# An attention kernel with an MLP behind it: a new order model, free choice of engine for copies, and zero-padded means

## The chip, the cores and the metric

The kernel runs on one core of one Trainium2 chip. The metric is the device time of the whole program in microseconds (us), median of three executions. The core has five engines that work side by side and wait for one another through semaphores: TensorE (PE in the profile, with its weight loads PEld), VectorE (DVE), ScalarE (ACT), GpSimd (POOL) and SyncE (SP, which here issues most DMAs). Matmul results go to PSUM; this kernel uses four tiles of two banks there: duo0, duo1, hps and ops.

## What is computed

Two attentions over the same q, k and v (8 batches, 8 heads, 576 positions, 64 per head) are added, and the sum goes through an MLP with a SiLU.

```python
q_d = q.reshape(B, H, Sd, 4, D).mean(axis=3)          # the same for k_d, v_d: 144 means of four rows
out_d = sm_attn(q_d, k_d, v_d)                         # softmax attention over the 144 means
out_up = np.repeat(out_d, 4, axis=2)
mask = np.abs(pos[:, None] - pos[None, :]) < 4         # a band of 7 positions
scores = np.where(mask, scale * q @ k.T, -1e9)
out_local = softmax(scores) @ v
x = (out_up + out_local)                               # (4608 tokens, 512)
h = x @ w_in                                           # 512 x 2048
out = (h * sigmoid(h)) @ w_out                         # 2048 x 512
```

## The kernel before

Heads are worked on in pairs (32 of them), two pairs make a quad (16). The names of the phases are those of the text that follows:

- c, T, o, m: cast q and k to bf16, transpose them (TQ, TK on PE for the first eight quads, by DMA for the other eight), copy into qT and kT, form the means qd and kd.
- S1, S2: scores. S1 and the first two matmuls of S2 are the band, in five windows of 128 keys; the rest of S2 are scores of the means.
- e1, e2, e3, k: exponentials on ScalarE into Pt (band) and Pd (means), and the band mask on VectorE.
- Z or ZD: sums of the exponentials on PE, for the softmax. The first four quads are "direct": ZD, the reciprocals and RB (a matmul that spreads them over the partitions) stay on chip. For the others the reciprocals rr go through DRAM (scr) and come back broadcast as Rb.
- VD or castv (cv): means of v, on PE for the direct quads, on GpSimd for the others, into vd.
- PV: the products with v; pa and pb multiply by Rb into xo, and ad adds the repeated mean part to the local part into xT on GpSimd.
- g1, th, st: the first MLP matmuls (hps), tanh, and the product into gT. g2, ob, out: the second MLP matmuls (ops), copy, store.

No order is written by hand. Every phase is a task of one engine, with the tasks that must come first; at build time a greedy scheduler keeps a model of when each engine and buffer is free, and takes the next task per engine by modelled start plus weights from a table. That fixes each engine's instruction stream; on the chip every engine runs its stream in order and waits on semaphores.

```python
def choose(eng):
    c = [(s, t) for t in Q[eng][:LOOK[eng]] for s in [start(eng, t)] if s is not None]
    if eng != "PE":
        ...
        return min(c, key=lambda x: P.ready(eng, x[1][3], ()) + TUNE.get(kind(x[1][0]), 0))
    lead = min(max(ng1[0] - 16 - ng2[0], -16), 16)
    c = [(s + TUNE[kind(t[0])] + (0 if t[5] == mode[0] else TUNE["mode"]), s, t) for s, t in c]
    for k, r, w in mlp():
        s = max(P.free["PE"], P.ready("PE", r, w))
        c.append((s + TUNE[k] + (TUNE["lead"] * lead * (1 if k == "g1" else -1)) + ..., s, k))
    return min(c, key=lambda x: x[0])[1:] if c else None
```

The phases on PE that the change touches. `mm(..., m=...)` names the shape in which the array is used; the model charges 95 ns when it changes.

```python
vd = sb("vd", [128, 3, 2, 64], BF16, NVD)      # means of v: pair a of the quad on rows 64a to 64a+47
Pd = sb("Pd", [128, 2, 3, 72], BF16, NP_)      # exponentials of the means

def ph_S2(p):
    ...                                         # two matmuls of the band, m="row"
    for i in range(3):
        for b in range(2):
            for h in range(2):
                rows = slice(64 * h, 64 * h + 64)
                mm(D[rows, b, 120 + 72 * i:192 + 72 * i], kd[j][rows, i:i + 190:3],
                   qd[j][rows, 72 * b:72 * b + 72], ..., cost=18, m="diag")

def ph_Z(z):
    for c in range(8):                          # four at a time, 128 rows
        for o, m, a in hd:
            mm(D[o:o + 32, 0, 0:72], onesZ[:, c, :], Pt[m][:, a, 72 * c:72 * c + 72], ..., m="col4")
    for c in range(6):                          # four at a time, 48 rows
        for o, m, a in hd:
            mm(D[o:o + 32, 0, 0:72], onesZ[64 * a:64 * a + 48, 8 + c // 3, :],
               Pd[m][64 * a:64 * a + 48, c // 3, c % 3, :], ..., m="diag4")

def ph_PV(p):
    for c in range(5):                          # ten matmuls, two at a time, 128 rows
        for h in range(2):
            mm(o, vb[n][:, 5 * h + c, :], Pt[ms[h]][:, a, QB[c]:QB[c] + NQ[c]], ..., m="col")
    rows = slice(64 * a, 64 * a + 48)
    for i3 in range(3):                         # six matmuls, two at a time, 48 rows
        for h in range(2):
            mm(D[64 * h:64 * h + 64, 1, 120:264], vd[nd][rows, i3, h, :],
               Pd[ms[h]][rows, :, i3, :], ..., m="diag")
```

Each copy, cast and mean has one fixed engine:

```python
def castw(p):                                   # v to bf16
    P.op("ACT", lambda e: e.activation(vb[m][:, :, :], t, AF.Copy), ..., cost=730)
def cast(p, nm):                                # q, k: GpSimd (the first two pairs: VectorE and ScalarE)
    pool(lambda g: g.tensor_copy(dst, t), ..., cost=650)
pool_mean = tuple(range(2, 8))                  # heads whose k mean is on GpSimd, all others VectorE
```

At the very start VectorE fills constants, 16 of them memsets of four columns each:

```python
for t, c in ((onesS, 1.0), (foursS, 4.0)):
    fill(t[:, :, :], 0.0, [R("osb1")], 100, over=c > 1)
    for y in range(8):
        fill(t[:, y, 4 * y:4 * y + 4], c, [R("osb1")], 60, over=True)
```

Of the kernel before, what the change touches and what calls it, by code (L numbers as in the profile page):

```python
# [19 lines left out]
TUNE = {  # L20
    "tol": 0, "mode": 139, "lead": 77, "rep": 204, "g1": 606, "g2": 650, "TQ": -272, "TK": -88, "VD": -803,
    "S1": 101, "S2": -85, "ZD": -9384, "Z": -112, "RB": -6751, "PV": -220, "cw": 3143, "cv": -1199, "cq": 2831,
    "ck": 2297, "mask": -3629, "neg": -5281, "dm": 3751, "ones": 4973, "Tq": 6872, "Tk": 6930, "mq": -13444,
    "mk": -645, "e1": 916, "e2": -5624, "e3": 2392, "k": -751, "rc": -14116, "zs": -6353, "rb": 5365,
    "pa": -2169, "pb": -943, "th": 696, "st": 302, "ob": -445, "oq": -5037, "ok": -1684, "ad": -10747,
    "lqk": 5289, "lv": -8757, "lvq": 7893, "r": -4373, "b": 6923, "tq": -1508, "tk": 378, "out": 3873,
    "seq": ["lqk0", "lqk1", "lqk2", "lqk3", "lv1", "lv0", "w3", "lqk5", "lv2", "w0", "lqk4", "lv3", "lqk7",
            "lv5", "lv4", "w1", "lqk6", "w2", "w5", "lv7", "lv6", "w7", "w4", "w6", "lqk9", "lqk8"],
# [22 lines left out]
class Prog:  # L51
# [9 lines left out]
    def __init__(self):  # L61
        self.streams = {e: [] for e in self.ENGS}
        self.know = {e: {} for e in self.ENGS}
        self.dcount = {}
        self.free = {e: 0 for e in self.ENGS}
        self.rings = {"SP": [], "POOL": [], "ACT": []}
        self.ring_t = 0
        self.tag = ""
# [29 lines left out]
    def ready(self, eng, r, w):  # L98

        t = 0  # L100
        for x in r:
            for o in (x.last.values() if x.psum else x.writers):
                if o.eng != eng or o.dsem:
                    t = max(t, o.end + self.LATENCY[o.eng])
# [20 lines left out]
    def op(self, eng, fn, r=(), w=(), dma=None, cost=0, issue=450, tau=90):  # L125
# [31 lines left out]
        else:  # L157
            op.t0 = t
            self.free[eng] = op.end = t + cost * (1.3 if eng == "PE" and t < 40000 else 1)
        op.deps = [d for d, f in deps]  # L160
# [63 lines left out]
def bass_hourglass_attn__then__act_silu_kernel(  # L224
# [9 lines left out]
    with kctx:  # L234
# [22 lines left out]
        NST, NSTV, NVB, NVD, NP_, NR, NQT = 3, 2, 5, 3, 6, 4, 3  # L257
# [7 lines left out]
        vd = sb("vd", [128, 3, 2, 64], BF16, NVD)  # L265
# [8 lines left out]
        Pd = sb("Pd", [128, 2, 3, 72], BF16, NP_)  # L274
# [8 lines left out]
        onesZ = sb("onesZ", [128, 10, 32], BF16)  # L283
# [5 lines left out]
        rsb = sb("rsb", [128, 270], BF16, 2)  # L289
# [7 lines left out]
        direct, by_dma = tuple(range(4)), tuple(range(8, NQUAD))  # L297
        pool_mean = tuple(range(2, 8))
# [11 lines left out]
        def const_id():  # L310
            fill(id_bf[:, :], 0.0, [R("id")], 100)
            fill(mask_bf[:, :], 1.0, [R("mask")], 200)
            fill(band[:, :, :, :], 1.0, [R("band")], 60)
            for t, c in ((onesS, 1.0), (foursS, 4.0)):
                fill(t[:, :, :], 0.0, [R("osb1")], 100, over=c > 1)
                for y in range(8):
                    fill(t[:, y, 4 * y:4 * y + 4], c, [R("osb1")], 60, over=True)
            fill(Dm[:, :, :, 0:48], 1.0, [R("Dm")], 450)
            fill(Dm[:, :, :, 48:64], 0.0, [R("Dm")], 180)
            for i in range(2):  # L320
                fill(kd[i][:, 144:192], 0.0, [R(f"kdz{i}")], 60)
                fill(vq[32:64, i, :, :], 0.0, [R("vqz")], 800)
            fill(onesZ[:, :, :], 0.0, [R("ones")], 120)
            fill(onesZ[:, 0, 30:32], 1.0, [R("ones")], 60, over=True)
            pool(lambda g: g.affine_select(out=id_bf[:, :], in_=id_bf[:, :], compare_op=ALU.not_equal,
                                           fill=1.0, base=0, pattern=[[-1, 128]], channel_multiplier=1),
                 r=[R("id")], w=[R("id")])

        def const_z():

# [652 lines left out]
```

The softmax here doesn't subtract the row's maximum and nothing guards it: scores larger than these inputs give would overflow.

## Time and profile before

| | before |
|---|---|
| time, median of three | 391.66 us (391.12 to 392.93) |
| span of the profiled execution | 389.2 us |
| TensorE busy | 354.7 us, 91% |
| VectorE, ScalarE, GpSimd busy | 239.6, 215.1, 136.9 us |
| mean granted TensorE clock | 0.969 |
| moved by DMA | 66.77 MB, mean 172 GB/s |

The page of the profile describes one execution. Its slices cut the span in 40 equal parts of 9.7 us, with a digit for the busy share in tenths. The chain of waits goes back from the last instruction, at each step to what released it. Groups put together the instructions of one source line. All tasks of PE come from one helper line, so they are told apart by the names of their tiles: `hps<-xT,w_in_sb` is g1, `ops<-w_out_bf,gT` g2, `duo<-Pt,vb` and `duo<-Pd,vd` PV, `duo<-Pt,onesZ` Z. Matmuls are pipelined, so their durations overlap, and their distances are read from start to start. Two helper rows more, as an example of how such a group is read:

```profile
L754 DVE SCALAR_TENSOR_TENSOR gT<-th,hps 128x512 bf16<-128x512 f32 x136 | 92.5, 682 | 87.6 <-ACT th L752 87.5
L752 ACT ACTIVATE th<-hps 128x512 f32<-128x512 f32 x136 | 81.2, 598 | 107.5 <-PE hps L481 107.3
```

VectorE forms gT 136 times from hps, 92.5 us busy in all and 682 ns each; before these it stood idle 87.6 us, nearly all of it waiting for ScalarE's tanh, which in turn waits for PE.

### The profile page before, as it was taken

What the parts mean: (1) busy time and instruction counts of PE and PEld (TensorE: products, weight loads), DVE (VectorE), ACT (ScalarE), POOL (GpSimd) and SP (SyncE); (2) the same over time, 40 slices, a digit from 0 to 9 for tenths busy, and PEclk for the clock granted to TensorE, in tenths of its full rate; (3) what the DMA queues carried; (4) which work ended last, traced back from release to release, by engine and by line L of the source; (5) the groups of instructions that cost most, each with busy time, mean ns of one, the idle gap of its engine ahead of it and who ended that gap; (6) DMA issues with size and microseconds to landing.
All of it is one profiled execution on the core that took longest, in us unless ns stands there. A gap on an engine that the chain in (4) does not pass through costs nothing.

```text
span 389.2 us, 9061 instructions
## 1 busy us (share of the span) xinstructions
PE 354.7 (91%) x3841; PEld 221.3 (57%) x3880; DVE 239.6 (62%) x394; ACT 215.1 (55%) x364; POOL 136.9 (35%) x173
## 2 busy tenths in 40 slices
PE   0768599898999999999699999999999999999996
PEld 0656476655655556556455655666555656556542
DVE  6927477779978775986558899654363433334310
ACT  4756367666656765786167768463424344344321
POOL 7746826377624533452534622550040000000000
PEclk9968699999999999999879999999999999999999
DMA  8998997699999999999999999964000101101012
GB/s 260 323 319 232 177 250 191 193 250 240 262 247 274 194 252 242 285 219 220 173 256 239 195 174 226 211 156 108 27 29 32 51 27 44 39 27 53 29 54 81
DMA packets 87464, 66.77 MB, mean 172 GB/s; under 512 B 65152, under 2 KB 67200, under 8 KB 87424
## 3 DMA queue, kind: packets, MB, share of 16 engines
q1 hardware_dynamic: 83200, 59.90, 66.1%
q0 software_dynamic: 4224, 6.29, 7.3%
q8 instruction: 30, 0.49, 0.6%
q14 instruction: 10, 0.08, 0.1%
HBM read 53.67 MB, written 9.88 MB: 163 GB/s over the span
## 4 chain that ended last, share of the span: by engine, by line
PE 76%; DVE 15%; DMA 5%; issue 3%; ACT 1%; DVEq 0%; ACTq 0%
PE hps L481 31%; PE ops L481 30%; PE duo L481 12%; DMA qr<-qb 5%; DVE qd L519 3%; DVE qT L388 3%; DVE gT L754 2%; DVE qT L499 2%; DVE Pt L556 2%; PE duo L491 1%; DVE kd L519 1%; PE ops L491 0%; DVE rr L577 0%; DVE osb L308 0%; DVE duo L655 0%
## 5 line engine op out<-in xcount | busy, mean ns | idle before, releaser
L481 PE MATMUL hps<-xT,w_in_sb 128*128 128x512 f32 x544 | 169.9, 437 | 4.1 <-DVE gT L754 3.9
L754 DVE SCALAR_TENSOR_TENSOR gT<-th,hps 128x512 bf16<-128x512 f32 x136 | 92.5, 682 | 87.6 <-ACT th L752 87.5
L481 PE MATMUL ops<-w_out_bf,gT 128*128 128x512 bf16 x537 | 137.6, 383 | 3.9 <-issue 2.4
L752 ACT ACTIVATE th<-hps 128x512 f32<-128x512 f32 x136 | 81.2, 598 | 107.5 <-PE hps L481 107.3
L481 PEld LDWEIGHTS hps<-xT,w_in_sb 128*128 128x128 f32 x544 | 101.3, 193 | 34.5 <-DVE gT L754 7.1
L481 PEld LDWEIGHTS ops<-w_out_bf,gT 128*128 128x128 bf16 x576 | 47.5, 98 | 68.3 <-issue 25.5
L731 POOL TENSOR_TENSOR xT<-xo 128x576 fp32r<-128x576 f32 (+2 forms) x40 | 39.9, 1018 | 73.1 <-DVE xo L714 73.0
L433 POOL TENSOR_TENSOR vq<-vq 112x768 f32<-112x768 f32 x12 | 22.4, 1868 | 37.4 <-DMA vq<-in_v_dram 37.4
L556 DVE TENSOR_TENSOR Pt<-Pt,mask_bf 128x1152 bf16<-128x1152 bf16 x32 | 28.1, 884 | 11.8 <-ACT Pt L548 11.7
L775 ACT ACTIVATE osb<-ops 128x512 f32<-128x512 f32 x36 | 21.5, 597 | 25.1 <-PE ops L481 24.9
L532 ACT ACTIVATE Pt<-duo 128x912 bf16<-128x912 f32 x28 | 26.0, 928 | 6.4 <-PE duo L481 6.3
L519 DVE TENSOR_REDUCE qd<-qT 128x144 bf16<-128x576 bf16 x32 | 24.1, 752 | 5.7 <-PE duo L481 4.5
L422 POOL CAST qb<-qs 128x576 bf16<-128x576 f32 x27 | 18.8, 705 | 22.9 <-PE duo L491 17.8
L427 ACT ACTIVATE vb<-vs 128x640 bf16<-128x640 f32 x30 | 21.8, 738 | 4.0 <-DMA vs<-in_v_dram 2.4
L422 POOL CAST kb<-ks 128x576 bf16<-128x576 f32 x27 | 18.8, 708 | 8.4 <-DMA kr<-kb 6.6
L711 DVE TENSOR_TENSOR xo<-duo,Rb 128x456 f32<-128x456 f32 x29 | 18.0, 628 | 5.0 <-PE duo L481 2.9
L388 DVE TENSOR_REDUCE qT<-qr 128x576 bf16<-128x576 bf16 x16 | 18.6, 1162 | 3.4 <-DMA qr<-qb 3.4
L519 DVE TENSOR_REDUCE kd<-kT 128x144 bf16<-128x576 bf16 x26 | 18.9, 741 | 1.3 <-ACT kT L391 1.3
L391 ACT ACTIVATE kT<-kr 128x576 bf16<-128x576 bf16 x16 | 19.1, 1221 | 0.1
L550 ACT ACTIVATE Pd<-duo 128x432 bf16<-128x432 f32 x30 | 16.0, 534 | 0.0
L481 PE MATMUL duo<-qd,kd 64*64 64x72 bf16 x360 | 14.2, 218 | 0.8 <-DVE kd L519 0.8
L481 PEld LDWEIGHTS duo<-qT,kT 64*128 64x128 bf16 x284 | 8.1, 95 | 11.9 <-issue 6.3
(119 smaller groups left out, 297.6 us busy)
## 6 DMA issues: line engine op xcount, KB each, us to landing
vs<-in_v_dram SPq DMA_DIRECT2D x60, 160.0 KB, 5.2
out_dram<-osb SPq DMA_DIRECT2D x36, 256.0 KB, 2.0
Rb<-scr SPq DMA_DIRECT2D x24, 360.0 KB, 6.8
qs<-in_q_dram SPq DMA_DIRECT2D x29, 288.0 KB, 6.2
ks<-in_k_dram SPq DMA_DIRECT2D x29, 288.0 KB, 6.2
vq<-in_v_dram SPq DMA_DIRECT2D x24, 288.0 KB, 6.3
w_in_sb<-in_moe_w_in_dram POOLq DMA_DIRECT2D x4, 1024.0 KB, 8.2
w_out_bf<-in_moe_w_out_dram POOLq DMA_DIRECT2D x4, 512.0 KB, 10.4
```

What stands on the lines that cost most here:

```text
L388: P.op("DVE", lambda e: e.tensor_reduce(dst, src.unsqueeze(3), mybir.AxisListType.X, ALU.add), r=[R("qr")], w=[R(f"qT{y}")], cost=745)
L422: pool(lambda g: g.tensor_copy(dst, t), r=rs_, w=w, cost=650)
L427: P.op("ACT", lambda e: e.activation(vb[m][:, :, :], t, AF.Copy), r=rs_, w=[R(f"vb{m}")], cost=730)
L433: pool(lambda g: g.tensor_tensor(t, t, z, ALU.add), r=[R("vq"), R("vqz")], w=[R("vq")], cost=1900)
L481: return P.op("PE", lambda t: t.matmul(out_, lhsT, rhs, start=start, stop=stop, skip_group_check=True), r, w, cost=cost)
L519: P.op("DVE", lambda e: e.tensor_reduce(dst[j][:, 0:144], src[y][:, :].rearrange("p (g r) -> p g r", r=4), mybir.AxisListType.X, ALU.add), ...
L532: later("ACT", f"e1{p}", [(lambda e: e.activation(Pt[m][:, :, 0:456], D[:, :, 0:456], AF.Exp, scale=0.125), bk, [R(f"P{m}")], 930)], bk)
L556: P.op("DVE", lambda e: e.tensor_tensor(Pt[m][:, :, :], Pt[m][:, :, :], mask_bf[:, :].unsqueeze(1).to_broadcast([128, 2, S_]), ALU.mult), ...
L731: P.op("POOL", lambda e, dst=dst, in0=in0, in1=in1: e.tensor_tensor(dst, in0, in1, ALU.add), r=[R(f"xo{x}")], w=xblk(kc, t, e_), cost=200 ...
L752: later("ACT", f"th{n}", [(lambda e: e.activation(th[tb][:, :], hp, AF.Tanh, scale=0.5), [hr], [R(f"th{tb}")], 597)], [hr], pre=[f"st{n - ...
L754: later("DVE", f"st{n}", [(lambda e: e.scalar_tensor_tensor(gT[j % 2][:, f, :], th[tb][:, :], 1.0, hp, ALU.add, ALU.mult), [hr, R(f"th{tb} ...
L775: later("ACT", f"ob{n}", [(lambda e: e.activation(osb[s_][:, :], ops[:, ob, :], AF.Copy, scale=0.5), [R(f"o{ob}", True)], [R(f"osb{s_}")], ...
```

## The change

The change has three parts.

First, the order model. It now knows that a GpSimd operation and certain VectorE operations (the mask product and the q and k casts) exclude each other ("lock"). It supposes that whatever comes by DMA is 1500 ns later than modelled when it ranks tasks ("late"), gives PE tasks 500 ns of slack once the MLP has begun, and favours the oldest pair ("age"). Modelled costs are brought nearer to the traced ones, and the weights and the order of the first loads are new.

Second, a copy, cast or mean may go to any of two or three engines; the scheduler takes the one that is free first.

Third, the means of v get a buffer for each pair of the quad, with zeros in the rows that belong to the other one, so that the matmuls can run over all 128 rows; the sums (Z) get weights with zeros likewise, and the layout of Pd is changed so that two of the three parts of the mean scores are done with matmuls of 144 columns.

Beside these, constants are filled in fewer memsets and as tasks, and the reciprocals of the direct quads live in osb0.

```diff
-    "tol": 0, "mode": 139, "lead": 77, "rep": 204, "g1": 606, "g2": 650, ...
+    "tol": 0, "mode": -162, "lead": 54, "rep": 260, "g1": 738, "g2": 894, ...
+    "late": 1500, "slack": 500, "slack1": 300, "direct": 4, "dma": 8, ... "age": 759, "alt": 1177,
@@ Prog
-    def ready(self, eng, r, w):
+    def ready(self, eng, r, w, late=0):
-                    t = max(t, o.end + self.LATENCY[o.eng])
+                    t = max(t, o.end + self.LATENCY[o.eng] + (late if o.dsem else 0))
+            if lock or eng == "POOL":
+                t = max(t, self.lock)
+        if lock or (eng == "POOL" and not dma):
+            self.lock = op.end
@@ buffers
-        NST, NSTV, NVB, NVD, NP_, NR, NQT = 3, 2, 5, 3, 6, 4, 3
+        NST, NSTV, NVB, NVD, NP_, NR, NQT = 3, 2, 5, 2, 6, 4, 3
-        vd = sb("vd", [128, 3, 2, 64], BF16, NVD)
+        vd = sb("vd", [128, 2, 3, 2, 64], BF16, NVD)
-        Pd = sb("Pd", [128, 2, 3, 72], BF16, NP_)
+        Pd = sb("Pd", [128, 2, 216], BF16, NP_)
@@ castv
-            pool(lambda g: g.tensor_tensor(vd[m][0:112, ...], x, y, ALU.add), ..., cost=1100)
+            for a, n in ((1, 112), (0, 48)):
+                pool(lambda g, a=a, n=n: g.tensor_tensor(
+                    vd[m][0:n, a, :, :, :].rearrange("p i h d -> p h i d"), x[0:n], y[0:n], ALU.add), ..., cost=1030)
+            pool(lambda g: g.memset(vd[m][0:64, 1, :, :, :], 0.0), ..., cost=400)
@@ ph_S2
-            for i in range(3):
-                for b in range(2):
-                    for h in range(2):
-                        mm(D[rows, b, 120 + 72 * i:192 + 72 * i], ..., cost=18, m="diag")
+            for i, b, lo, hi in ((0, 0, 0, 144), (1, 1, 0, 144), (2, 0, 0, 72), (2, 1, 72, 144)):
+                for h in range(2):
+                    mm(D[rows, b, x:x + hi - lo], ..., qd[j][rows, lo:hi], ..., cost=31 if i < 2 else 22, m="diag")
@@ ph_Z
-                    mm(D[o:o + 32, 0, 0:72], onesZ[64 * a:64 * a + 48, 8 + c // 3, :], ..., m="diag4")
+                    mm(D[o:o + 32, 0, 0:72], onesZ[:, 8 + 2 * a + y, :], rhs, ..., m="col4")
@@ ph_PV
-                    mm(D[64 * h:64 * h + 64, 1, 120:264], vd[nd][rows, i3, h, :], Pd[ms[h]][rows, :, i3, :], ..., m="diag")
+                    mm(D[64 * h:64 * h + 64, 1, 120:264], vd[nd][:, a, i3, h, :], ..., m="col")
@@ tasks
-            task("ACT", f"cw{p}", ...)
+            task(("ACT", "POOL"), f"cw{p}", ...)
-                task("POOL" if p >= 2 else "DVE" if x == "q" else "ACT", f"c{x}{p}", ...)
+                task(("POOL",) if i >= len(direct) else ("POOL", "DVE", "ACT"), f"c{x}{p}", ...)
-                        task("DVE" if x == "q" else "ACT", f"o{x}{s}", ...)
+                        task(("DVE", "ACT") if x == "q" else ("ACT", "DVE"), f"o{x}{s}", ...)
-                    task("POOL" if s in pool_mean and x == "k" else "DVE", f"m{x}{s}", ...)
+                    task(("DVE", "POOL") if i in direct else ("DVE",), f"m{x}{s}", ...)
@@ start, choose
+            s = P.ready(eng, t[3], w, TUNE["late"])
+            if eng == "PE" and ng1[0]:
+                s += TUNE["slack"]
+            if eng == "POOL" or (eng == "DVE" and kind(t[0]) in ("k", "cq", "ck")):
+                s = max(s, P.lock + (0 if eng == "POOL" else 60))
```

(Cut: the later_copy helper that does the same for copies out of PSUM (oq, ok, rb, cv, ob), the constants, the remaining costs and weights.)

## The prediction

> **What bounds the kernel now.** I read the page first (slices, chain of waits, groups), then the windows by stage, then the PE timeline and the chain in order of time where the slices dip.
>
> ```profile
> PE 354.7 (91%) x3841; PEld 221.3 (57%) x3880; DVE 239.6 (62%) x394; ACT 215.1 (55%) x364; POOL 136.9 (35%) x173
> ...
> PE   0768599898999999999699999999999999999996
> ...
> PEclk9968699999999999999879999999999999999999
> ...
> PE 76%; DVE 15%; DMA 5%; issue 3%; ACT 1%; DVEq 0%; ACTq 0%
> ```
>
> TensorE (PE) is the bound, but not everywhere: its row is ragged for the first five slices (0 to 49 us), then 9 except for slice 19 (185 to 195 us), and the clock row dips in the same two places. So there are three pools of time: the start, one hole in the middle, and a stretch where each nanosecond of PE work counts.
>
> ```profile
> 0.00:46.30 46.30, 26.03 (x742) 21.78 (x743) 29.55 (x75) 25.25 (x44) 31.80 (x60) 0.84 1.00 267
> 46.30:100.00 53.70, 49.85 (x665) 33.94 (x667) 41.66 (x63) 36.72 (x69) 29.00 (x35) 0.98 0.93 228
> 100.00:200.00 100.00, 94.69 (x1115) 57.09 (x1123) 74.85 (x114) 63.46 (x105) 43.00 (x49) 0.97 1.12 234
> 200.00:300.00 100.00, 98.58 (x958) 60.05 (x970) 65.57 (x104) 56.80 (x94) 33.08 (x31) 1.00 0.69 148
> 300.00:389.20 89.20, 85.56 (x376) 48.47 (x382) 27.93 (x41) 32.84 (x55) 0.00 (x0) 1.00 0.12 45
> ```
>
> Windows by stage (PE, PEld, DVE, ACT, POOL busy, clock, DMA share, GB/s). The first MLP matmul starts at 46.3 us; before it PE is busy 26 of 46 us, and no engine is full: latency sets that stage. From 100 to 200 us the DMA engines are full (share 1.12). The last 89 us are the MLP alone at two groups of four matmuls (0.93 and 0.88 us) per 1.81 us, which the change does not touch.
>
> PE timeline, one sum (Z) and one output phase (PV) between MLP groups (start, us, operation):
>
> ```profile
> 222.27 0.44 PE L481 MATMUL duo<-Pt,onesZ 128*32 128x72 bf16 x32
> 222.64 0.38 PE L481 MATMUL duo<-Pd,onesZ 48*32 48x72 bf16 x24
> 222.95 1.19 PE L481 MATMUL hps<-xT,w_in_sb 128*128 128x512 f32 x4
> ...
> 228.69 0.44 PE L481 MATMUL duo<-Pt,vb 128*64 128x120 bf16 x10
> 229.06 0.38 PE L481 MATMUL duo<-Pd,vd 48*64 48x144 bf16 x6
> 229.37 0.44 PE L481 MATMUL duo<-Pt,vb 128*64 128x120 bf16 x10
> ```
>
> Starts count here, as durations overlap. Z issues its matmuls four abreast: 8 quads and one change of tile shape take 222.64 - 222.27 = 0.37 us, 6 quads and one change 222.95 - 222.64 = 0.31. Hence a quad is (0.37 - 0.31) / 2 = 0.03 us and a change of shape 0.37 - 8 x 0.03 = 0.13. PV fits with the same 0.13: five pairs over about 116 columns (0.37 - 0.13) / 5 = 0.048, three pairs over 144 columns (0.31 - 0.13) / 3 = 0.06, in proportion to the columns.
>
> The hole, from the chain in order of time (start, us, what):
>
> ```profile
> 177.11 11.05 DMA qr<-qb
> ...
> 188.18 1.17 DVE qT L388
> ...
> 190.13 1.03 DVE qT L388
> 191.16 0.02 issue
> 191.19 0.75 DVE qd L519
> 191.94 0.61 DVE gT L754
> 192.54 0.04 issue
> 192.59 3.78 PE hps L481 x8
> ```
>
> A transposing DMA lands 11 us after its issue; VectorE's queue is in order, so two reorderings and two means (188.2 to 191.9) stand ahead of the gT that frees a PSUM bank. PE idles 2.9 us, and then eight matmuls take 3.78 us instead of 1.86, the next eight 3.05 instead of 1.81. The hole costs 2.9 + 1.9 + 1.2 = 6.0 us.
>
> **What the Trainium skill says.**
> - "TensorEngine Tiling (Array Packing)", Tiling Modes, Key Properties: changing the tiling mode, not just the tile, drains the TensorE. The trace agrees, at the 0.13 us above.
> - "TensorE: Matmul & The Clock Gate", HAM oscillation: a long enough idle gap drops the PE to half clock. The trace agrees: after the 2.9 us idle the clock averages 0.70 and 0.62 in the next two 5 us windows. The page speaks of gaps above about 3 us; here 2.9 did it.
> - "Advanced Engine Details and Errata", VectorE Performance Modes: VectorE's second SBUF port is shared with GpSimd, and the two block each other. The trace shows something like it: the mask product on VectorE has a median of 755 ns and a maximum of 2200, GpSimd casts 667 and up to 1243. The old order knew nothing of this; the new one charges for it.
> - "GPSIMD Engine Reference", Engine selection: two-input work is about twice as slow there as on VectorE. Here a mean costs 663 + 425 ns on GpSimd against 752 on VectorE, 1.4 times.
>
> **The change part by part.** Most of it alters the scheduler that fixes each engine's order at build time, so I read the new order off the built program.
>
> *Zero-padded v means.* PV's last six matmuls and Z's last 24 use all 128 rows, so they keep the shape of those before them: one change of shape less each, 0.13 us. Rows are free on PE, columns are not. After the first MLP matmul 28 PV and 12 Z remain: 40 x 0.13 = 5.2 us. In S2, twelve matmuls of 72 columns become four of 144 and four of 72: today 0.39 us from first to next phase (220.75 to 221.14), so a 72-column pair is (0.39 - 0.13) / 6 = 0.043; new 2 x 0.06 + 2 x 0.043 + 0.13 = 0.336; saved 0.054, on 26 S2 phases 1.4 us. The PE-bound stretch loses 6.6 us of work. The price is on GpSimd: per indirect quad one more add (about 1.12 us, as the old one) and a short memset.
>
> *Copies and casts on whichever engine is free.* GpSimd gets 16 v casts (0.74 us, an estimate from ScalarE's row) = +12, loses 8 q/k casts (0.70) = -6, gains 12 adds = +13 and 12 memsets, for which I allow +4: about 160 us from 137. ScalarE loses those 16 casts, 8 output copies and 5 Rb copies and gains 11 qT copies and 8 reorderings, about -10; VectorE ends within a few us of today. None is near full on average, so this is worth something only where a queue is late.
>
> *Start.* Before, PE has 3 ZD, 6 RB, 4 PV and six heads' scores ahead of its first MLP matmul; after, 2 ZD, 4 RB and the rest the same. Today that third ZD and its RB run from 41.5 to 46.3 us with 2.1 us of waiting for the reciprocal chain. VectorE's 18 tiny memsets (1.6 to 4.1 us) become 4, and the first casts, which today wait for all memsets until 7.4 us, go to ScalarE and GpSimd. I put the first MLP matmul at about 42 us, 4 earlier. The displaced ZD and RB cost 2.0 us of PE later: net -2.
>
> *Spread.* Scores end in MLP block 7 (g1 group 112) rather than 6, and means, loads and transposes spread likewise. A DMA-fed task is now assumed 1.5 us later than modelled, and PE tasks are given 0.5 us of slack. That aims at the hole. I credit 5 of its 6.0 us. Entries into attention from an MLP group, where the timeline shows about 0.1 to 0.2 us of extra start delay, stay at 66 but shift away from the dearer g1 side (42 to 36): -0.6.
>
> Sum: -6.6 - 2 - 5 - 0.6 = -14.2, and +3 for new holes, since a new order meets delays it was not made for: 391.7 - 11.2 = 380.5 us.
>
> **Rivals.**
> 1. *Reciprocals become the late thing.* In the new order PV follows its Z by only nine or ten MLP groups (about 10 us) in the last four quads, and again in the second; before it was 17 us or more everywhere. The path between is rr, the write to scr (3 to 4 us landing, typically) and two Rb broadcasts (median 6.8 us): with issue about 12 us. If the DMA engines stay as full as between 100 and 200 us, VectorE waits 2 to 3 us at the xo product in five quads, with gT behind it. One or two us of that the second hps bank absorbs. For it: the slack. Against: by the last quads DMA is quieter (the last pair landed 3.9 and 4.8 us after issue). Worst case +8 to +10: about 389.
> 2. *GpSimd or the shared port.* Its load rises by a sixth and its adds feed xT, which must be ready one to five us after the last PV of a batch. Today it waits 73 us for xo and is busy 43 of 100 us in the fullest window, so I expect it to keep up. If not, +3 to +5: 385.
> 3. *The start stays.* The 4.0 us PE idle from 19 to 23 us has no visible releaser ("issue"), probably instruction supply beside full DMA queues; it may move, not vanish, and a hole of 3 us brings half clock with it. Then only packing and the hole are gained: 383.
> 4. *Only packing.* The hole is replaced by one of equal size: 384 to 385.
>
> **Range and chances.** The packing gain is nearly sure (6 us, 1.6%); 2% is 7.8 us, so a third more must come from start or hole. All good: 374. Rival 1 in full: 389. So 373 to 389, 380.5 as the middle; faster by over 2% at 0.65, within 2% 0.30, slower 0.05.
>
> **What would show it.** Packing: in the PE timeline PV's starts 0.55 us apart instead of 0.68, Z 0.55 instead of 0.68, and no 48-row matmuls but those of ZD. Start: first w_in_sb matmul before 44 us. Hole: no gT wait of over 1.5 us on PE and a clock row at 9 after the first five slices. Rival 1: VectorE waiting on "DMA Rb<-scr" for over 6 us in all (2.0 today). Rival 2: PE or VectorE waiting on POOL xT. I am wrong if PE idles in sum as long after 46 us as today (about 14 us).

## The result and the profile after

| | before | after |
|---|---|---|
| time, median of four | 391.96 us (391.12 to 392.93) | 382.27 us (381.35 to 383.65) |
| ratio, 95% interval | | 0.9755 (0.9712 to 0.9798) |
| span of the profiled execution | 389.2 us | 381.3 us |
| PE busy; mean granted clock | 354.7 us; 0.969 | 348.2 us; 0.977 |
| VectorE, ScalarE, GpSimd busy | 239.6, 215.1, 136.9 us | 243.2, 211.4, 160.3 us |
| first `w_in_sb` matmul | 46.3 us | 41.5 us |
| PE not busy after 46 us | 14.2 us | 13.6 us |

The changed kernel is 9.7 us (2.5%) faster; 11.2 had been predicted (391.66 us, given for the kernel before further up, is the median of the first three of the same four executions). The last line of the table is the remarkable one: behind the start PE stands idle as long as before. It is even somewhat longer, as the trace of the kernel before lacks 39 of the 576 matmul records of the second MLP matmuls, and the 2.4 us of "issue" ahead of it are probably their gaps:

```profile
L481 PE MATMUL ops<-w_out_bf,gT 128*128 128x512 bf16 x537 | 137.6, 383 | 3.9 <-issue 2.4
```

The lines of the changed kernel's page that answer to those of the kernel before (busy times, the slices of PE and of its clock, the chain by engine):

```profile
PE 348.2 (91%) x3752; PEld 218.4 (57%) x3752; DVE 243.2 (64%) x390; ACT 211.4 (55%) x352; POOL 160.3 (42%) x209
...
PE   1675869999896999999999999999999999999996
...
PEclk9987989999999899999999999999999999999999
...
PE 82%; DVE 6%; ACT 5%; POOL 4%; issue 3%; POOLq 0%; DVEq 0%; ACTq 0%
```

The dip of PE that stood in slice 19 is gone, and a dip of PE stands in slice 12 (114 to 124 us), with clock at 8 a little later. GpSimd, which was not on the chain at all, has 4% of it. The windows by stage (PE, PEld, DVE, ACT, POOL busy, clock, DMA share, GB/s):

```profile
0.00:41.50 41.50, 23.31 (x574) 19.55 (x574) 26.02 (x58) 24.67 (x43) 25.29 (x55) 0.88 0.97 278
41.50:100.00 58.50, 50.93 (x762) 33.99 (x758) 44.34 (x70) 36.76 (x66) 33.26 (x40) 0.97 0.89 204
100.00:200.00 100.00, 95.92 (x973) 59.36 (x968) 71.79 (x109) 56.02 (x92) 53.29 (x64) 0.98 1.02 236
200.00:300.00 100.00, 100.00 (x1094) 61.42 (x1090) 74.47 (x116) 64.85 (x104) 45.98 (x51) 1.00 0.74 162
300.00:381.30 81.30, 78.07 (x374) 44.12 (x368) 26.53 (x40) 29.14 (x49) 2.44 (x2) 1.00 0.11 43
```

From 200 to 300 us the trace shows no idle PE. What is left to gain lies ahead of that: 18 us not busy up to 41.5 us, 7.6 from there to 100 us and 4.1 from there to 200 us.

**The packed phases.** The PE timeline, one Z and then a couple of PV (start, us, operation):

```profile
108.76 0.44 PE L523 MATMUL duo<-Pt,onesZ 128*32 128x72 bf16 x32
109.02 0.37 PE L523 MATMUL duo<-Pd,onesZ 128*32 128x72 bf16 x24
109.32 0.97 PE L523 MATMUL hps<-xT,w_in_sb 128*128 128x512 f32 x3
...
230.00 0.44 PE L523 MATMUL duo<-Pt,vb 128*64 128x120 bf16 x10
230.27 0.35 PE L523 MATMUL duo<-Pd,vd 128*64 128x144 bf16 x6
230.46 0.42 PE L523 MATMUL duo<-Pt,vb 128*64 128x120 bf16 x10
230.71 0.35 PE L523 MATMUL duo<-Pd,vd 128*64 128x144 bf16 x6
231.00 2.10 PE L523 MATMUL hps<-xT,w_in_sb 128*128 128x512 f32 x8
```

Z goes from first start to the next phase in 109.32 - 108.76 = 0.56 us (0.68 before), a couple of PV in 231.00 - 230.00 = 1.00 us. The second PV of the couple takes over the shape of the first, so it saves a change at its beginning as well.

**A wait that moved.** Before, PE idled 4.0 us up to 23.0 us with "issue" as its releaser. Now there are two long waits of that kind. Timelines of PE, one line of the kernel before, then the changed kernel:

```profile
23.00 0.37 PE L481 MATMUL ops<-qT,kT 64*128 64x112 bf16 x3 [4.02 <-issue]
```

```profile
18.16 1.53 PE L523 MATMUL duo<-vb,Dm 128*64 128x128 bf16 x30
19.63 0.21 PE L523 MATMUL duo<-osb,gT 128*128 128x90 bf16 x1
22.59 0.66 PE L523 MATMUL duo<-osb,gT 128*128 128x90 bf16 x7 [2.75 <-issue]
...
49.51 0.47 PE L523 MATMUL duo<-vb,Dm 128*64 128x128 bf16 x10
53.49 1.28 PE L523 MATMUL duo<-vb,Dm 128*64 128x128 bf16 x20 [3.51 <-issue]
```

Both stand in the middle of a phase, after one of 8 and after 10 of 30 matmuls, so an operand is hardly what was awaited. The second is new, and lies in the stretch where the MLP already runs: 3.5 us idle, then half clock for 3.4 us, which costs half of that, 1.7: 5.2 us in all.

**A hole that GpSimd makes.** The chain in order of time (start, us, what) over the new dip:

```profile
114.13 0.39 PE duo L523 x10
...
114.65 0.72 POOL vb L381
115.37 1.81 POOL vq L462
...
117.31 1.95 POOL vd L464 x2
...
119.32 0.41 POOL vd L467
119.73 1.22 POOL kb L381 x2
120.95 2.63 POOL xT L768 x4
...
123.67 0.63 DVE xo L748
124.30 0.35 DVE xo L751
...
124.70 0.58 PE duo L523 x9
```

GpSimd runs its queue in order. At its head stood a cast of v into vb, waiting since 104.8 us for the PV that frees the buffer. Behind it came the means of v, casts of k and only then the additions that empty xo; VectorE waits for those at xo, PE for VectorE. PE idles 0.83 + 0.30 + 1.90 + 0.57 = 3.6 us between 117 and 124 us and then has 3.4 us of half clock: 5.3 us. Only the waits of 1.90 and 0.57 us end with xo and so hang on GpSimd; the first two end with ScalarE's kT and Pt.

### The profile page after: what moved, and what is told of

Same layout as the page of the kernel before. It is cut to its first block, busy times and chain, and to the rows that moved or that the text cites. A ratio compares the mean times of both kernels' runs of the same rounds, so it can differ in the third digit from the quotient of the medians.

```text
span 381.3 us, 8872 instructions
## 1 busy us (share of the span) xinstructions
PE 348.2 (91%) x3752; PEld 218.4 (57%) x3752; DVE 243.2 (64%) x390; ACT 211.4 (55%) x352; POOL 160.3 (42%) x209
## 4 chain that ended last, share of the span: by engine, by line
PE 82%; DVE 6%; ACT 5%; POOL 4%; issue 3%; POOLq 0%; DVEq 0%; ACTq 0%
PE ops L523 34%; PE hps L523 33%; PE duo L523 12%; PE duo L533 2%; DVE Pt L593 2%; POOL xT L768 1%; ACT kT L377 1%; ACT Pt L570 1%; DVE kd L557 1%; DVE gT L791 1%; POOL mask_bf L369 1%; DVE qd L557 1%; POOL vd L464 1%; ACT gT L641 1%; POOL vq L462 0%
## 5 line engine op out<-in xcount | busy, mean ns | idle before, releaser
L523 PE MATMUL hps<-xT,w_in_sb 128*128 128x512 f32 x544 | 163.9, 430 | 1.3 <-POOL xT L768 1.2
L523 PE MATMUL ops<-w_out_bf,gT 128*128 128x512 bf16 x576 | 143.4, 381 | 0.0
L593 DVE TENSOR_TENSOR Pt<-Pt,mask_bf 128x1152 bf16<-128x1152 bf16 x32 | 30.8, 964 | 4.0 <-ACT Pt L585 2.3
L377 ACT ACTIVATE osb<-ops 128x512 f32<-128x512 f32 x28 | 16.8, 599 | 29.4 <-PE ops L523 29.3
L381 POOL CAST vb<-vs 128x640 bf16<-128x640 f32 x15 | 11.2, 758 | 40.5 <-PE duo L523 40.5
L464 POOL TENSOR_TENSOR vd<-vq 112x384 bf16<-112x384 f32 (+1 forms) x24 | 23.9, 1019 | 1.3
L557 DVE TENSOR_REDUCE kd<-kT 128x144 bf16<-128x576 bf16 x31 | 22.6, 747 | 2.1 <-ACT kT L377 1.8
L557 DVE TENSOR_REDUCE qd<-qT 128x144 bf16<-128x576 bf16 x27 | 20.1, 748 | 1.1 <-ACT qT L377 0.4
L523 PE MATMUL duo<-qT,kT 64*128 64x112 bf16 (+1 forms) x298 | 14.9, 218 | 4.8 <-DVE xo L748 2.5
L533 PE MATMUL duo<-id_bf,qb 128*128 128x128 bf16 x63 | 6.4, 261 | 9.3 <-ACT qb L377 8.1
## 6 DMA issues: line engine op xcount, KB each, us to landing
w_in_sb<-in_moe_w_in_dram POOLq DMA_DIRECT2D x4, 1024.0 KB, 11.8
```

Source lines behind the costliest of these rows:

```text
L377: fn = lambda e: e.activation(dst, src, AF.Copy, scale=1.0 if scale is None else scale)
L381: fn = lambda e: e.tensor_copy(dst, src)
L464: pool(lambda g, a=a, n=n: g.tensor_tensor(vd[m][0:n, a, :, :, :].rearrange("p i h d -> p h i d"), x[0:n], y[0:n], ALU.add), r=[R("vq"), R ...
L523: return P.op("PE", lambda t: t.matmul(out_, lhsT, rhs, start=start, stop=stop, skip_group_check=True), r, w, cost=cost)
L557: P.op("DVE", lambda e: e.tensor_reduce(dst[j][:, 0:144], src[y][:, :].rearrange("p (g r) -> p g r", r=4), mybir.AxisListType.X, ALU.add), ...
L593: P.op("DVE", lambda e: e.tensor_tensor(Pt[m][:, :, :], Pt[m][:, :, :], mask_bf[:, :].unsqueeze(1).to_broadcast([128, 2, S_]), ALU.mult), ...
```

## The experiments

The ratios are of undisturbed runs on both sides, so they need not equal the ratio of the medians given beside them. What a run is compared with is the changed kernel's 382.27 us, or the kernel before. The kernel before was run again beside each experiment, the changed kernel was not; the kernel before took 391.96 us beside the changed kernel and 389.5 to 390.5 us (medians) beside the experiments. So a difference of 1 to 3 us from 382.27 counts only where the interval of the ratio lies clear of the changed kernel's (0.9712 to 0.9798), or where a trace shows it.

**1. The packing undone (a_rows48).** The changed kernel, order as it is, PV and Z over 48 rows again:

```diff
-mm(D[64*h:64*h+64, 1, 120:264], vd[nd][:, a, i3, h, :], t[:, i3, 0:144] ...)
+rows = slice(64*a, 64*a + 48)
+mm(D[64*h:64*h+64, 1, 120:264], vd[nd][rows, a, i3, h, :], t[rows, i3, 0:144] ...)
```

> The changed kernel with its instruction order untouched on every engine, but PV's last six matmuls and Z's last 24 over 48 rows again, as before (the output stays the same, as the other rows are zeros). Theory (packing): each change of array shape costs 0.13 us, and beside the two that I counted per PV the second PV of a couple again has to change back, since two PV in a row now keep one shape: 12 Z x 0.13 + 32 PV x 0.13 + 16 couples x 0.1 = 7 us, of which some lies in waits of the first 41 us: +5 to +7 us, 387 to 389; PV couples 1.36 us from start to end in the timeline instead of 1.0. Rival (the packing only fills waits that the order has anyway): +0 to +2 us.

Measured: 388.95 us, 6.7 above the changed kernel; against the kernel before 1.0009 (0.9981 to 1.0036). PE timeline, the couple of PV that was shown above:

```profile
233.20 0.44 PE L523 MATMUL duo<-Pt,vb 128*64 128x120 bf16 x10
233.57 0.38 PE L523 MATMUL duo<-Pd,vd 48*64 48x144 bf16 x6
233.88 0.44 PE L523 MATMUL duo<-Pt,vb 128*64 128x120 bf16 x10
234.25 0.37 PE L523 MATMUL duo<-Pd,vd 48*64 48x144 bf16 x6
234.56 2.12 PE L523 MATMUL hps<-xT,w_in_sb 128*128 128x512 f32 x8
```

1.36 us instead of 1.00, in the same place of the same order. From the 33rd MLP group (125.6 us here, 126.1 in the changed kernel) to the 129th (340.7 and 335.0) it takes 215.1 us instead of 208.9: 6.2 us in the PE-bound stretch. So the packing of PV and Z is worth 6 to 7 us. All that the rest of the change (the new order, the free choice of engine and S2's 144 columns) brings on top is 0 us by the ratio and 3.0 by the medians.

**2. The packing alone (b_before_rows128).** The kernel before, with its order, PV and Z over all 128 rows. It leaves out the zero padding: the added rows bring in means and weights of the other pair.

```diff
-mm(D[64*h:64*h+64, 1, 120:264], vd[nd][rows, i3, h, :], Pd[ms[h]][rows, :, i3, :] ...)
+mm(D[64*h:64*h+64, 1, 120:264], vd[nd][:, i3, h, :], Pd[ms[h]][:, :, i3, :] ...)
```

> The kernel before with its order untouched, but the same matmuls of PV and Z over all 128 rows of the old buffers. It leaves out the zero padding, so the means of the two pairs of a quad are mixed in the output; only the time counts. Packing alone, without the new order: theory -5 to -7 us, 385 to 387, and the hole at 190 us and the first MLP matmul at 46 us stay where they are. Rival: another wait takes its place, -2 us or less. Together with the run above it gives the part of the new order alone: theory 3 to 5 us.

Measured: 387.87 us, ratio to the kernel before 0.9931 (0.9908 to 0.9954): 2.7 us, about half of what theory had. Its first MLP matmul comes 1.5 us later than before, the hole stays (2.85 us up to 193 us), and new gaps of 1.0 and 1.7 us stand at 175 and 223 us. PE work that is saved in the old order seems to be partly turned into waits for what feeds it. Two things disturb the reading: a new "issue" wait of 1.3 us stands at 29.7 us, in the midst of a ZD, and the hole is not followed by half clock here, while that of the kernel before is.

**3. The means' scores in twelve matmuls (c_s2_twelve).**

```diff
-for i, b, lo, hi in ((0, 0, 0, 144), (1, 1, 0, 144), (2, 0, 0, 72), (2, 1, 72, 144)):
+for i, b, lo, hi in ((0, 0, 0, 72), (0, 0, 72, 144), (1, 1, 0, 72), (1, 1, 72, 144), (2, 0, 0, 72), (2, 1, 72, 144)):
```

> The changed kernel, order untouched, with S2's means again in twelve matmuls of 72 columns instead of four of 144 and four of 72. Theory: 0.054 us per S2, 32 of them: +1.7 us, 384. Rival (128 more matmuls also bring more fetches of instructions, which are what the idle PE at 20, 34 and 50 us waits for): +3 us or more, with those idle stretches at other places in the program.

Measured: 379.51 us, ratio 0.9712 (0.9663 to 0.9760). More work and 2.8 us faster by the median (the ratios' intervals overlap), in no case the 1.7 us slower that were expected, and no wait on data explains it. In the trace the "issue" waits are of 2.11 and 0.82 us only, and the one at 50 us is gone. Counting what PE's queue shows in the trace from the first on ("records": matmuls, weight loads and the few semaphore instructions among them), the two stand at records 451 and 962. Those of the changed kernel stand at 451, 963 and 1475, that of the kernel before at 452. The additional matmuls had put other work at the same counts.

**4. 64 tiny matmuls ahead (d_pad64).** The changed kernel; PE is idle there anyway, until 8.0 us.

```diff
         const_id()
+        for _ in range(64):
+            P.op("PE", lambda t: t.matmul(hps[0:32, 0, 0:8], id_bf[:, 0:32], id_bf[:, 0:8], start=True, stop=True), ...)
```

> The changed kernel with 64 tiny matmuls (32 columns of weights, 8 of data) put ahead of everything on PE, where it idles until 8 us anyway; nothing else moves. In the trace of the changed kernel PE idles with no visible releaser before its records number 451 (2.7 us), 963 (1.2) and 1475 (3.5), exactly 512 records apart, and each time an instruction packet of 16 KB had landed 1.4 to 1.7 us before PE went on. Theory (supply of instructions): with 128 more instructions ahead, the idle stretches move 128 instructions back in the program, into the three ZD phases. Rival (a wait of these phases that the profile does not show): they stay before RB, TQ and VD. Time: 379 to 385 under both; less if the early matmuls also wake the PE clock, so that the first nine transposes take 0.5 us instead of 0.9.

Measured: 373.95 us (373.37 to 374.26), ratio 0.9564 (0.9495 to 0.9633): 8.3 us below the changed kernel, below the 379 to 385 us of both theories, and the fastest complete version of this study. Slices of PE and clock on its page:

```profile
PE   3668899899987999999999999999999999999996
PEclk9996999999998999999999999999999999999999
```

Slice 5, which had 6, has 9. The "issue" waits are 0.43 us at record 707 and 0.65 at 962, no more (2.75, 1.21 and 3.51 us in the changed kernel). The dip that GpSimd makes stays (now 109 to 115 us).

**5. The same for the kernel before (e_before_pad64).**

> The kernel before, unchanged but for 64 tiny matmuls (8 columns each, results never read) ahead of everything on TensorE, in the 8.9 us in which it waits for its first input. Theory A (TensorE runs dry at a fixed count of its own instructions, 512 records apart, and 64 matmuls with their 64 weight loads move that point by 128 records): the 4.0 us of idle time at record 452 (19.0 to 23.0 us) shrinks to under 1 us or moves, the half clock from 21.3 to 28.1 us goes with it, the first w_in_sb matmul comes at 41 to 44 us instead of 46.3, and the time falls by 4 to 8 us against the kernel before, to 384 to 388 us. Theory B (the early wait of the kernel before comes from its order of work, which the change mended): the wait stays where it is in the work (between ops<-qT,kT matmuls), and the time stays within 1 us of 391.5.

Measured: 392.28 us, ratio 1.0083 (1.0057 to 1.0108): 0.8% slower than the kernel before, where a gain of 4 to 8 us was expected. The wait did move, but no gain came of it. Timeline of PE:

```profile
26.76 0.66 PE L481 MATMUL duo<-Pt,osb 128*32 128x72 bf16 x30
27.35 0.82 PE L481 MATMUL duo<-Pd,osb 48*32 48x18 bf16 x82
31.90 0.28 PE L481 MATMUL duo<-Pd,osb 48*32 48x18 bf16 x14 [3.73 <-issue]
```

It now stands at record 962, in the midst of a ZD, with others of 1.48 us at record 450 and 0.79 at 1474: 6.0 us in all instead of 4.0, and the first MLP matmul comes at 50.4 us instead of 46.3. The count is what stays, the work under it changes; whether that is better is chance. The prediction of a gain was wrong, that of the mechanism right. With the same 64 matmuls ahead of both kernels the changed one is 18.3 us faster (392.28 and 373.95), without them 9.7.

**6. 128 tiny matmuls (h_pad128).**

> The changed kernel with 128 tiny matmuls instead of 64 ahead of everything on TensorE (about 3.7 us of the 8.0 that it waits there), order otherwise the same. Theory A (an instruction block boundary stalls TensorE where it has just run through a stretch of many short matmuls; what counts is the place of the boundary): the boundaries fall at records 195, 707 and 1219 of the changed kernel's count; 707 lies behind the wait for onesS at 32.2 us, 195 inside the VD matmuls at about 16 us and 1219 in the first MLP matmuls; the time lies between 372 and 379 us and idle gaps, if any, stand at those records. Theory B (the 64 matmuls helped because they warm the clock or hold TensorE busy at the start): 128 do at least as well as 64, and the gaps stay at the places in the work where they were with 64.

Measured: 384.92 us, ratio 0.9856 (0.9790 to 0.9922), 2.7 us above the changed kernel (the intervals just overlap) and far above d_pad64. Timeline of PE:

```profile
49.20 0.47 PE L523 MATMUL duo<-vb,Dm 128*64 128x128 bf16 x10
54.11 1.17 PE L523 MATMUL duo<-vb,Dm 128*64 128x128 bf16 x18 [4.44 <-issue]
```

After 10 of 30 matmuls of the same phase: exactly where the changed kernel stops. The waits are at records 707, 1219 and 1731, which is 451, 963 and 1475 plus the 256 records of 128 tiny matmuls and their weight loads. As waits stand at 451, 707 and 963 in one kernel or another, the period is 256 records: a shift by 256 leaves them where they were in the work, and theory B (tiny matmuls help because they warm PE up) is out. My expected time was wrong since I had taken the period for 512.

The page counts 29 packets, 0.48 MB, in the queue of kind "instruction": 16 KB each. In the trace they land 1.3 to 1.7 us before PE resumes (at 20.9, 33.8 and 52.1 us in the changed kernel, for waits that end at 22.6, 35.3 and 53.5). The Trainium skill, "Runtime: NRT & Kernel Launch", Instruction fetch mechanics, says that instructions come in blocks of 16 KiB or 256, the next one fetched while the current one runs; of the crossing it says "mostly hidden". The size agrees; hidden it is not here. For some of the crossings, how long the 256 records before it had run, start to start, and the gap between the two starts at it:

| kernel, record | 256 records before ran | gap |
|---|---|---|
| h_pad128, 1219 | 1.5 us | 1.8 us |
| changed kernel, 963 | 1.6 | 1.5 |
| before, 451 | 1.7 | 4.2 |
| e_before_pad64, 963 | 2.1 | 3.9 |
| i_pad32, 451 | 2.1 | 2.6 |
| e_before_pad64, 2243 | 2.3 | none |
| changed kernel, 1475 | 2.5 | 3.7 |
| h_pad128, 1731 | 2.5 | 4.7 |
| changed kernel, 451 | 3.4 | 3.0 |
| f_cv_short, 451 | 3.6 | 2.3 |
| j_pad80, 1219 | 4.8 | 1.2 |
| j_pad80, 707 | 5.6 | 1.7 |
| d_pad64, 963 | 6.7 | 0.8 |
| changed kernel, 707 | 9.6 | none |

All gaps over 2 us, in all runs, follow a block that ran in at most 3.6 us, but not every such block is followed by one. After 1.6 us the changed kernel's gap is 1.5, after 1.7 us that of the kernel before is 4.2, and e_before_pad64 has none after 2.3 us (at 73 us); what decides this stays open. The fastest blocks are those with all or most of a ZD in them: its 128 matmuls with their weight loads are as many records as a whole block, and PE runs through them in 1.2 to 1.5 us. (i_pad32, j_pad80 and f_cv_short are described below.)

**7. 32 and 80 tiny matmuls (i_pad32, j_pad80).** From the table I made a rule, wait = 6 us less the run of the block before, and tried it on two other shifts.

> The changed kernel with 32 tiny matmuls ahead on TensorE. Worked out from the runs so far: block boundaries lie at records 195 + 256k of TensorE's stream in every kernel run, and at each the wait is about 6 us less the time in which the last 256 records ran (451 in the changed kernel: 3.35 us, wait 2.96; 1475: 2.52, wait 3.73; 834 of the kernel before with 64: 2.14, wait 3.91). Theory A (that rule): with 32 the boundaries move to records 387, 899 and 1411 of the changed kernel's count, so waits of about 3.5, 4.1 and 1.6 us at records 451, 963 and 1475 of this run, nothing at the others; time within 2 us of the changed kernel's 382.3, not near 374. Theory B (any small number of tiny matmuls helps at the start): below 377.

> The changed kernel with 80 tiny matmuls. By the rule of 6 us for a block, worked out on the records of the changed kernel, 80 is the best number between 0 and 127: the one wait left is of about 1.2 us at record 1059 of the changed kernel's count (1219 of this run), and none at 707 or 963. Theory A: time 372.5 to 374.5 (64 gave 373.95), and PE's idle time up to the first w_in_sb matmul at most that with 64 less the tiny matmuls' own time. Theory B (64 was a lucky draw in the order of DMA packets): anywhere from 374 to 383.

Measured: 377.78 us with 32 (ratio 0.9683, 0.9625 to 0.9741), 377.01 us with 80 (0.9648, 0.9602 to 0.9695). The rule fails as a rule, and both times lie outside theory A. With 32 the waits are 2.3 us at record 450 and 0.4 at 962 instead of 3.5 and 4.1, none at 1475; with 80 there are 1.4 us at 707, where none was expected, and 1.0 at 1219, where 1.2 was. The places are right each time; how long the wait there is, the count and the run of the block before do not settle. By number of tiny matmuls the changed kernel takes:

| 0 | 32 | 64 | 80 | 128 |
|---|---|---|---|---|
| 382.27 | 377.78 | 373.95 | 377.01 | 384.92 us |
| 0.9755 | 0.9683 | 0.9564 | 0.9648 | 0.9856 of the kernel before |

**8. ZD thinned out (k_zd_third).** It leaves out two of the three sums over the means in each ZD, so the early quads' denominators lack them. No tiny matmuls.

```diff
-for i3 in range(3):
+for i3 in range(1):
```

> The changed kernel without two of the three matmuls in each mean sum of the early quads: it leaves out those sums over the second and third column group (the denominators of the early quads are then too small), 457 of the first 2000 records of TensorE, all of them matmuls of 18 or so columns at 12 ns each; order otherwise the same, no tiny matmuls ahead. By the rule of 6 us for a block, no block runs faster than it is fetched then. Theory A (dense short matmuls outrun the fetch of instructions): no wait at records 451, 963 and 1475, the first w_in_sb matmul at 36 to 39 us instead of 41.5, time 373 to 378, of which 2.7 us are the matmuls left out. Theory B (the waits belong to DMA queues full of loads at 20 and 50 us, whatever TensorE runs): waits of 2 to 4 us remain at about 20 to 22 and 50 to 53 us, time 378 to 381.

Measured: 370.08 us (369.45 to 370.53), ratio 0.9473 (0.9435 to 0.9511). PE runs through the place of the changed kernel's first wait:

```profile
17.62 1.82 PE L523 MATMUL duo<-vb,Dm 128*64 128x128 bf16 x30
19.37 0.49 PE L523 MATMUL duo<-osb,gT 128*128 128x90 bf16 x8
19.70 0.48 PE L523 MATMUL hps<-osb,gT 128*128 128x90 bf16 x8
```

No wait of this kind is left at any block (none of them ran in under 5.8 us), though DMA is as full as before (share 1.04 over the first 38 us), and the first MLP matmul comes at 36.2 us. Theory A holds, though the time is 3 us below its range: where the dense short matmuls are thinned out, PE no longer runs out of instructions. Of the 12.2 us about 2.3 are the matmuls left out (the 96 of a ZD take 0.86 us in d_pad64: two thirds, four times), so the waits and what followed them cost the changed kernel 9 to 10 us, an estimate (the ratios, 0.9473 and 0.9755, give 9).

**9. GpSimd's hole (f_cv_short, g_pad64_cw13).** First, castv without its 48-row addition and memset, which leaves those means wrong:

```diff
-for a, n in ((1, 112), (0, 48)):
+for a, n in ((1, 112),):
...
-pool(lambda g: g.memset(vd[m][0:64, 1, :, :, :], 0.0), ...)
```

> The changed kernel, same order on every engine but for one exchange of two DMA issues, without the 48-row addition and the memset of castv: it leaves out 1.4 us of GpSimd work for each of the twelve quads by the sum (rows of the second diagonal group then hold wrong means). Theory A (the hole at 117 to 124 us is made by GpSimd, whose cast of vb waited 9.8 us for TensorE and pushed the additions, the casts of kb and the xT additions back): the hole shrinks by about 1.4 us and perhaps loses its half clock, xT waits on VectorE of 7.4 us in sum fall to about 4, and the time falls by 1.5 to 3.5 us against the changed kernel's 382.3. Theory B (GpSimd's lateness there is hidden behind the exponentials, which have 1.8 us of their own wait): under 0.7 us.

Measured: 381.08 us, ratio 0.9751 (0.9691 to 0.9811), 1.2 us below the changed kernel by the median and the same by the ratio; 1.5 to 3.5 us were expected. Timeline of PE in the hole:

```profile
120.79 0.90 PE L523 MATMUL duo<-qT,kT 64*128 64x120 bf16 x8 [0.26 <-DVE xo L748]
122.07 0.62 PE L523 MATMUL duo<-qT,kT 64*128 64x120 bf16 x2 [0.38 <-DVE xo L748]
```

The waits of 1.90 and 0.57 us are 0.26 and 0.38, so GpSimd's work in front of xT does make them. From the 17th MLP group to the 33rd it takes 38.5 us instead of 41.2, which is 2.7 us less, but half clock comes all the same, for 6.8 us from 120 us, and the wait at 50 us was followed by 6.8 us of half clock instead of 3.4.

Then, with 64 tiny matmuls, the cast of the fourteenth pair given to ScalarE:

```diff
-task(("ACT", "POOL"), f"cw{p}", ...)
+task("ACT" if p == 13 else ("ACT", "POOL"), f"cw{p}", ...)
```

> The changed kernel with the 64 tiny matmuls, and with the cast of vb of the fourteenth pair given to ScalarE instead of whichever engine the model finds free: this cast stood first in GpSimd's queue from 95.3 us and waited 9.8 us for TensorE. The scheduler runs anew, so some hundred places in the order change, all after about 95 us. Theory A (head of the queue blocked on GpSimd makes the hole at 109 to 115 us of the kernel with the 64 matmuls, 3.3 us idle and 1.7 us lost to half clock): the hole and its half clock go, 373.95 becomes 369 to 371.5 us. Theory B (GpSimd simply has too much work in this stretch): it moves by a few us and the time stays at 373 to 375.

Measured: 376.07 us, ratio 0.9624 (0.9554 to 0.9694), 2.1 us above d_pad64 (the intervals overlap), and not the 369 to 371.5 us of theory A. The scheduler put another cast of vb in the same place:

```profile
105.84 0.72 POOL L381 CAST vb<-vs 128x640 bf16<-128x640 f32 x1 [10.26 <-PE duo L523]
```

It waits 10.3 us instead of 9.8, and four waits of 0.6 to 1.6 us follow between 114 and 124 us, without half clock. So this run doesn't tell the two theories apart; that a blocked head of the queue is the cause, rather than too much work, is argued from the chain and not shown.

**10. The order without the lock (l_pad64_nolock).** d_pad64 with the lock taken out of the scheduler's model; the operations are the same, but some go to another engine (GpSimd is busy 153.5 us instead of 159.8).

```diff
-            if lock or eng == "POOL":
-                t = max(t, self.lock)
...
-                s = max(s, P.lock + (0 if eng == "POOL" else 60))
```

> The changed kernel with 64 tiny matmuls, with the model of the lock between VectorE and GpSimd taken out of the scheduler (operations and their number unchanged; some 300 places in TensorE's order move). Against the kernel with 64 tiny matmuls, 373.95. Theory A (the model of the lock puts VectorE's operations where GpSimd does not hold the port, and the order needs it): the reductions and additions on VectorE stretch more often, time 376 to 381. Theory B (the weights of the order are tuned to a level at which the lock model adds nothing): 373 to 376. As the weights were found with the lock model in place, a loss of a few us is no proof of the model's worth by itself; only stretched VectorE operations in the profile would be.

Measured: 408.68 us, ratio 1.0458 (1.0403 to 1.0513), 34.7 us slower than with the lock in the model. The group of mask products on VectorE, first here, then in d_pad64:

```profile
L591 DVE TENSOR_TENSOR Pt<-Pt,mask_bf 128x1152 bf16<-128x1152 bf16 x32 | 35.3, 1105 | 15.0 <-ACT Pt L583 12.4 <-ACT Pt L568 2.4
```

```profile
L593 DVE TENSOR_TENSOR Pt<-Pt,mask_bf 128x1152 bf16<-128x1152 bf16 x32 | 29.2, 913 | 4.4 <-ACT Pt L585 2.8 <-ACT Pt L570 1.6
```

They stretch more often (mean 1105 ns instead of 913), but that is 6 us of VectorE's time. The loss is spread: PE is not busy for 53.2 us of the span instead of 24.3. The longest single wait comes of a chain near the end, in order of time:

```profile
328.06 1.06 PE duo L521 x55
...
329.14 0.62 DVE rr L613
...
329.77 2.33 DMA scr<-rr
...
332.74 5.42 DMA Rb<-scr
```

The last Z comes so late that reciprocals, write and broadcast lie open: PE idles 8.6 us up to 340.5 us. That is an order which the weights were not made for; how much the lock model would be worth with weights of its own wasn't tried.

## Why the prediction was right, and where not

The time, 380.5 us predicted, was right within 1.8 us, and its largest term, the packing, stands by its mechanism. That the rest came out so near is in part luck. The new holes cost several us more than allowed, and where the blocks of instructions fall, which no term of the sum held, moves the changed kernel between 373.95 and 384.92 us.

- *Packing, -6.6: right.* Z 0.56 us, one PV 0.56 to 0.57, a couple 1.00 where two single savings would give 1.10. Undoing PV and Z cost 6.2 us in the PE-bound stretch (run 1), of which 0.5 is idle time that came along; predicted were 5.2 for them, without the saving at the head of a couple's second PV; S2 takes 0.33 to 0.34 us to the next phase, 0.336 predicted. "Nearly sure" holds for this order only: in the old one it brought 2.7 (run 2).
- *Start, -2: the marker right, the gain not kept.* The first MLP matmul came at 41.5 us, predicted 42. But rival 3 came true in its mechanism: the 4.0 us wait was instruction supply, and it moved; its 383 us is also nearer to the 382.27 than the middle of the range. At the 17th MLP group the changed kernel is 1.3 us behind the kernel before (84.9 and 83.6 us).
- *The hole at 190 us, -5: right for the hole, not for the idle time as a whole.* PE doesn't wait there any more, and its clock stays full. But the idle time came back earlier: from the 33rd to the 129th MLP group PE is not busy for 0.1 us instead of 6.1, from the first to the 33rd for 11.5 instead of 4.8. The transposing DMAs land in a median of 4.4 us instead of 7.2; whether the spread work, the allowance for late DMAs or the slack did it was not tried separately.
- *New holes, +3: the term that was too small.* The one in which GpSimd is late cost 5.3 us (rival 2, which was given 3 to 5; 2.5 of its 3.6 us idle hang on GpSimd), the wait at 50 us 5.2 us: 10.5 together. The two profiled executions differ by 7.9 us (389.2 and 381.3), and -6.2, -1.4 for S2, -2, -6 and -0.6 add to -16.2, which leaves 8.3 for new holes; the 2 us between this and 10.5 I have not located. My own test, PE idle as long after 46 us as before, came out against me: 13.6 us and 14.2, or rather 11.8 without the gaps of the missing records. What fell in that stretch is PE's work, not its waiting.
- *Entries, -0.6:* too small to be seen beside the rest.
- *Rival 1: no.* VectorE's idle time ahead of xo is 9.7 us, of which 7.4 are for xT on GpSimd; 0.5 for Rb. In d_pad64 VectorE does wait 6.0 us for Rb, but from 117 to 296 us no idle time is left on PE, so it costs nothing there. In run 10 exactly this rival appears, with 8.6 us of idle PE.
- *GpSimd's load, 160 us predicted:* 160.3. The load on average was right and said nothing of the moment when it was late.

## What to carry to other kernels

A wait marked "issue" in the middle of a run of equal matmuls is hardly a wait for data: count the engine's instructions up to it in two kernels. If the counts agree modulo 256 (here within one or two), suspect instruction supply, and test it with a shift. Many short matmuls in a row can be dear for this reason (whether full DMA queues are needed for it wasn't tested). Any edit ahead of them moves the waits, here by several microseconds either way, so compare versions at two or three paddings before a gain or loss of 1 to 3% is ascribed to the edit itself. A task given to an engine because it is free on average can still block that engine's in-order queue: look at what stands behind its longest wait, not at its busy share.

## What the runs showed of the hardware

- PE's instructions arrive in packets of 16 KB, and PE can run dry at every 256th matmul or weight load. The gaps reached 4.7 us, all those over 2 us after blocks that ran in at most 3.6 us.
- 64 matmuls whose results nobody reads made the changed kernel 8.3 us faster (ratio 0.9564 against 0.9755); with 128 nothing of that was left (0.9856).
- A couple of phases in one array shape saves 0.36 us where one alone saves 0.12 to 0.13.
- Idle gaps of 0.3 to 1.9 us close together were followed by half clock (0.66 over 125 to 130 us in the changed kernel), not only single gaps of 3 us. No rule comes of it: gaps of 0.6 to 1.6 us in g_pad64_cw13 were not, and of two nearly equal holes the one of 2.9 us in the kernel before was, that of 2.85 us in b_before_rows128 was not.
